# Threshold attention and a feed-forward block: where a group's last addition, the second unit's products, the sums of w_ch1 and the variance stand

## The chip, the cores and the metric

The kernel runs on one core of a Trainium2 chip. The engines are TensorE (PE), VectorE (DVE), ScalarE (ACT), GpSimd (POOL) and SyncE (SP), which issues most DMAs. Each engine takes its instructions in the order in which they were written and waits for others by semaphores. The metric is the device time of one execution in microseconds; lower is better.

## The reference

Eight batches, eight heads, 576 positions, head size 64, all in float32. Attention keeps only the scores within tau of the row's maximum. Its output, with the heads side by side as 512 features, goes through a normalisation and two matrix products with a residual.

```python
scores = scale * np.matmul(q, k.transpose(0, 1, 3, 2))
thresh = np.max(scores, axis=-1, keepdims=True) - tau
scores = np.where(scores >= thresh, scores, -1000000000.0)
attn = np.exp(scores - np.max(scores, axis=-1, keepdims=True))
attn = attn / (np.sum(attn, axis=-1, keepdims=True) + 1e-09)
x = np.matmul(attn, v)          # then (B,H,S,D) -> (B,S,512)
mu = np.mean(x, axis=-1, keepdims=True)
var = np.mean((x - mu) ** 2, axis=-1, keepdims=True)
xn = (x - mu) / np.sqrt(var + 1e-06) * g_ln
out = x + np.maximum(xn @ w_ch1, 0.0) @ w_ch2   # 512 -> 2048 -> 512
```

## The kernel before

**Slots.** Attention runs in 72 slots, nine per batch. A slot makes the scores of one pair of heads (L417, written to the two PSUM tiles sc[0] and sc[1]), their negated row maxima on VectorE (`neg`, L450), thresholds on GpSimd (`thr`, L454), exponentials on ScalarE (`e`, L463), masks with row sums on VectorE (L473), the reciprocal (L478), the division on GpSimd (L490), and transposes on VectorE (L559), whose result goes to DRAM and back by DMAs on SP (`scr`, then `em`). One slot later TensorE multiplies `em` with the values (L638, L649) into the last bank of sc[0] and sc[1], and ScalarE copies that to x (L663).

**Groups.** The feed-forward block works on 16 groups of 288 positions, two per batch: an even one and an odd one. `group_ready` (L1298) files a group's preparation by slot and quarter: the mean, the centring (`centre`, L733, `xc`), the differences t1 to t4 (`sum_x`, L883; t4 on GpSimd), the squares for the variance (L1311) and their additions on GpSimd (L976). `ffn_steps` is a generator that yields after each product; `second_part` (L1249) draws from it in the four quarters of each slot, so that TensorE has feed-forward products between attention's. A yield's first number says where drawing may stop (4: it stops here).

**First product of a group.** `first_units` (L978) computes 2048 features as eight plain tiles (`p1`, one PSUM bank of the pool `ps_ff`, which has two) and two units (`unit`, L901). A unit computes four tiles with seven products instead of eight by sums of w_ch1's blocks, made once by `sums_of_w1` (L862) into `extra` while group 1 is in its second product, and by t1 to t4. Its products go to `chain` (a bank that is added to and copied by ScalarE in between: L929, L942, L948, L958), to `p2` and to two regions of sc[0] called `other`. Their additions on VectorE (L935) wait in `sums_due` until the slot's transposes are written. The two units of a group lie in two slots one after the other. After unit 0 `variance` (L964) writes an averaging product into a bank of its own and spreads it to the 128 partitions by four ScalarE instructions (L716), then Ln and Exp. In an odd group the first of the two slots also turns the next q and k (L355, on VectorE); in an even group the second does.

**Second product of a group.** `second_quarters` (L1072) does it with seven segments. Their additions on VectorE and GpSimd stand in the list `drops`, by name: "11", "21", "22", "u4", "hi" (multiply and add of half of y on GpSimd), "12" (adds the last segment's part p3, on VectorE), "done12" (GpSimd), and the stores. `drip` takes them out in order where a quarter has room; `sum_x` for t4 first takes drops until "12" of the group before is done, as t4 uses that part's buffer.

The pools give a buffer again once its readers are done, and the instruction that writes it waits for them by semaphore.

Of the kernel before, what the change touches and what calls it, by code (L numbers as in the profile page):

```python
# [8 lines left out]
F32 = mybir.dt.float32  # L9
# [3 lines left out]
ALU = mybir.AluOpType  # L13
# [5 lines left out]
def kernel(  # L19
# [31 lines left out]
    nc = tc.nc  # L51
# [5 lines left out]
    NK = DM // 128  # L57
# [646 lines left out]
    def average(to, bank, rhs, start, bias=None):  # L704


        for h in range(2):
            nc.tensor.matmul(
                bank[64 * h : 64 * h + 64], lhsT=avg_sb[:, 64 * h : 64 * h + 64],
                rhs=rhs[:, (early, late)[h]], start=start, stop=True, skip_group_check=True,  # L710
            )

        def spread():
            for at in range(2):
                for h in range(2):
                    nc.scalar.activation(  # L716
                        to[64 * at : 64 * at + 64, (early, late)[h]], bank[64 * h : 64 * h + 64],
                        func=AF.Identity, **({"bias": bias[64 * h : 64 * h + 64]} if bias is not None else {}),
                    )

        return spread
# [29 lines left out]
    def drip(room=None, everything=False):  # L751
# [5 lines left out]
        while drops:  # L757
# [6 lines left out]
            n -= 1  # L764
            go()

    def run_first(calls):
        for fn in calls[:1]:
            calls.pop(0)
            fn()  # L770
# [91 lines left out]
    def sums_of_w1():  # L862


        for k, (f1, f2) in enumerate(UNITS):
            for c in range(2):
                for m in range(2):
                    cols = [slice(128 * t[m], 128 * t[m] + 128) for t in (f1, f2)]
                    a11, a12 = (w1_sb[2 * j + c][:, cols[0]] for j in range(2))
                    a21, a22 = (w1_sb[2 * j + c][:, cols[1]] for j in range(2))  # L870
                    p2, p3, p4 = (piece_of(k, i, c, m) for i in range(3))
                    for eng, out, a, b, op in (
                        (nc.gpsimd, p3, a11, a21, ALU.subtract),
                        (nc.vector, a21, a21, a22, ALU.add),
                        (nc.vector, p2, a21, a11, ALU.subtract),
                        (nc.gpsimd, p4, a12, p2, ALU.subtract),
                    ):
                        eng.tensor_tensor(out=out, in0=a, in1=b, op=op)
                    yield
# [21 lines left out]
    def unit(g, xc, k):  # L901


        f1, f2 = UNITS[k]
        t1, t2, t3, t4 = sums_of_x[g]
        of = lambda f, j: hidden[:, f[0] : f[0] + 2, (early, late)[j]]
        h11, h12, h21, h22 = of(f1, 0), of(f1, 1), of(f2, 0), of(f2, 1)
        w_of = lambda f, j: lambda c, m: w1_sb[2 * j + c][:, 128 * f[m] : 128 * f[m] + 128]
        s_of = lambda which: lambda c, m: piece_of(k, which, c, m)
        x_of = lambda i, j: lambda c: xc[:, 2 * i + c, (early, late)[j]]  # L910
        t_of = lambda t: lambda c: t[:, c]
        other = [
            sc[0][:, 512 * i : 512 * i + TOK].rearrange("p (m t) -> p m t", m=2) for i in range(2)
        ]

        def steps(bank, lhs, rhs, first, last):
            for c in range(2):
                for m in range(2):
                    product(
                        bank[:, m], lhsT=lhs(c, m), rhs=rhs(c),  # L920
                        start=first and c == m == 0, stop=last and c == m == 1,
                        skip_group_check=True,
                    )
                    yield c == m == 1

        chain = ps_ff.tile([128, 2, HT], F32, tag="ff", name="chain")
        for _ in steps(chain, w_of(f1, 0), x_of(0, 0), True, False):
            yield 3, 0.5
        nc.scalar.copy(h12, chain)  # L929
        p2 = ps_ff.tile([128, 2, HT], F32, tag="ff", name="p2")  # L930
        for _ in steps(p2, w_of(f1, 1), x_of(1, 0), True, True):
            yield 3, 0.5

        def add(out, a, b):
            ins = nc.vector.tensor_tensor(out=out, in0=a, in1=b, op=ALU.add)  # L935
            if any(a is t for t in other):
                other_reads.append(ins.ins)

        sums_due.append(lambda: add(h11, p2, h12))
        for end in steps(chain, s_of(0), t_of(t2), False, False):  # L940
            yield 4 if end and part < 2 and now < QUARTERS * NS else 3, 0.5
        nc.scalar.copy(h22, chain)  # L942
        for _ in steps(other[0], w_of(f2, 0), t_of(t1), True, True):
            yield 3, 0.5
        sums_due.append(lambda: add(h12, other[0], h22))
        for _ in steps(chain, s_of(1), t_of(t3), False, False):
            yield 3, 0.5
        nc.scalar.copy(h21, chain)  # L948
        sums_due.append(lambda: add(h22, other[0], h21))
        for end in steps(other[1], s_of(2), x_of(1, 1), True, True):  # L950
            if end:
                sums_due.append(lambda: add(h12, other[1], h12))
            yield 4 if end and now < QUARTERS * NS else 3, 0.5
        for end in steps(chain, w_of(f2, 1), t_of(t4), False, True):
            if not end:
                yield 3, 0.5
        run_all(sums_due)
        nc.scalar.activation(h21, chain, func=AF.Relu)  # L958
        both = hidden[:, f1[0] : f1[0] + 2]
        nc.scalar.activation(both, both, func=AF.Relu)  # L960
        nc.scalar.activation(h22, h22, func=AF.Relu)
        yield 2 if k else 3, 0.5

    def variance(g, sq):  # L964
        x = spare.pop(g)
        bank = ps_ff.tile([128, HT], F32, tag="ff", name="var")
        average(x, bank, sq[:, 0], True, eps_sb)()
        rb = ffn.tile([128, TOK], F32, tag="rb", bufs=2, name="rb")
        nc.scalar.activation(rb, x, func=AF.Ln)
        nc.scalar.activation(rb, rb, func=AF.Exp, scale=-0.5)  # L970
        at_quarter(now // QUARTERS + 1, 3, root, rb, x)
        return rb
# [5 lines left out]
    def first_units(g):  # L978


        xc = centred[g]
        plain, slots = PLAIN[:], unit_slots(g)
        sq = hidden[:, ND - NK :]
        k = 0
        while plain or k < len(UNITS):
            if k < len(UNITS) and (not plain or now // QUARTERS >= slots[k] and part > 1):
                yield from unit(g, xc, k)
                k += 1
                if k == 1:
                    rb = variance(g, sq)  # L990
                    yield 2, 0.5
                continue
            d = plain.pop(0)
            p1 = ps_ff.tile([128, TOK], F32, tag="ff", name="p1")
            for c in range(NK):
                product(
                    p1, lhsT=w1_sb[c][:, d * 128 : (d + 1) * 128], rhs=xc[:, c],
                    start=(c == 0), stop=(c == NK - 1),
                )
                if c < NK - 1:  # L1000
                    yield 1, 1
            nc.scalar.activation(hidden[:, d], p1, func=AF.Relu)  # L1002
            yield 2, 1
        sums_of_x.pop(g)
        return rb
# [229 lines left out]
    def at_quarter(n, i, fn, *args):  # L1235
        later_calls.setdefault((n, i), []).append((fn, args))
# [61 lines left out]
    def group_ready(g):  # L1298
        first = divmod(ready(g), QUARTERS)
        before = divmod(ready(g) - 1, QUARTERS) if g else first  # L1300
        if g == 1:
            at_quarter(*before, lambda: among.append(g))
        else:
            at_quarter(*before, mean_of, g)
            at_quarter(*(first if g and first[1] else before), centre, g)
            if g > 1:
                sq = hidden[:, ND - NK :]
                at_quarter(*before, sum_x, g, (0, 1, 2))
                at_quarter(
                    first[0], -3,  # L1310
                    lambda: nc.scalar.activation(sq, centred[g], func=AF.Square),  # L1311
                )
                at_quarter(first[0], -1, add_squares, sq, 1, 2)
                at_quarter(first[0], 1, add_squares, sq, 3)
                at_quarter(first[0], 1, sum_x, g, (3,))
        at_quarter(*first, lambda: queue.append(ffn_steps(g)))
# [193 lines left out]
```

## Time and profile before

| what | value |
|---|---|
| median of 3 runs | 1337.48 us (1334.98 to 1338.02) |
| the profiled execution's own time | 1336.1 us |
| its span, first to last instruction | 1334.0 us |
| TensorE busy | 1285.2 us, 96% |
| VectorE, GpSimd, ScalarE busy | 947.3, 640.9, 515.0 us |
| granted TensorE clock, mean | 0.997 |

A row of the timeline gives start, duration (both us, from the span's start), engine, line of the kernel, operation, what it writes and reads, shapes, and in brackets the idle time before it and what ended it. Instructions alike that follow each other are one row with a count. Matmuls overlap, and the printed end of one is modelled. A row of the waits gives the waiting engine and line, what it waited for, microseconds in total, how many times, and the longest.

### The profile page before, as it was taken

What the parts mean: (1) busy time and instruction counts of PE and PEld (TensorE: products, weight loads), DVE (VectorE), ACT (ScalarE), POOL (GpSimd) and SP (SyncE); (2) the same over time, 40 slices, a digit from 0 to 9 for tenths busy, and PEclk for the clock granted to TensorE, in tenths of its full rate; (3) what the DMA queues carried; (4) which work ended last, traced back from release to release, by engine and by line L of the source; (5) the groups of instructions that cost most, each with busy time, mean ns of one, the idle gap of its engine ahead of it and who ended that gap; (6) DMA issues with size and microseconds to landing.
All of it is one profiled execution on the core that took longest, in us unless ns stands there. A gap on an engine that the chain in (4) does not pass through costs nothing.

```text
span 1334.0 us, 43429 instructions
## 1 busy us (share of the span) xinstructions
PE 1285.2 (96%) x18648; PEld 1052.7 (79%) x18648; DVE 947.3 (71%) x1714; ACT 515.0 (39%) x1163; POOL 640.9 (48%) x866
## 2 busy tenths in 40 slices
PE   8899899899999999999999999999999999999997
PEld 7765457779788897888879797888978888797977
DVE  7879886676777677777867767776777768676223
ACT  5866332242433424343342424334243433434130
POOL 3465555644445354454634454453544545344323
PEclk9999999999999999999999999999999999999999
DMA  8937765356744665545745566446655466454211
GB/s 155 300 107 187 199 167 182 120 167 193 196 152 148 189 170 169 183 142 148 208 152 188 146 188 194 152 149 189 173 172 178 131 162 186 153 188 143 56 19 19
DMA packets 335311, 214.11 MB, mean 161 GB/s; under 512 B 247376, under 2 KB 292688, under 8 KB 327056
## 3 DMA queue, kind: packets, MB, share of 16 engines
q1 hardware_dynamic: 329008, 210.46, 54.3%
q8 instruction: 146, 2.39, 0.8%
q10 hardware_dynamic: 5952, 0.74, 0.4%
q0 software_dynamic: 160, 0.15, 0.1%
q14 instruction: 45, 0.37, 0.1%
HBM read 124.00 MB, written 87.29 MB: 158 GB/s over the span
## 4 chain that ended last, share of the span: by engine, by line
PE 72%; DVE 8%; POOL 7%; SPq 4%; ACT 4%; issue 3%; DMA 2%; POOLq 0%; DVEq 0%; ACTq 0%
PE seg L103 29%; PE p L103 15%; PE sc L434 9%; PE sc L638 7%; PE chain L103 6%; PE sc L103 3%; POOL e L490 2%; DVE neg L450 2%; ACT e L463 2%; PE sc L649 2%; SPq L120 1%; DVE e L473 1%; DVE extra L569 1%; DVE hidden L935 1%; DVE e L559 1%
## 5 line engine op out<-in xcount | busy, mean ns | idle before, releaser
L103 PE MATMUL p<-xc,w 128*64 128x288 f32 (+1 forms) x2752 | 327.2, 389 | 11.6 <-ACT hidden L958 4.8
L450 DVE TENSOR_REDUCE neg<-sc 128x2 f32<-128x1152 f32 x144 | 189.5, 1353 | 149.8 <-PE sc L434 147.7
L103 PEld LDWEIGHTS p<-xc,w 128*64 128x64 f32 x2752 | 187.7, 137 | 133.4 <-issue 13.5
L490 POOL TENSOR_SCALAR e<-e,den 128x576 f32<-128x576 f32 x264 | 204.5, 788 | 83.5 <-DVE den L478 83.4
L103 PE MATMUL seg<-hidden,w 128*64 128x144 f32 x3840 | 243.9, 287 | 0.0
L103 PEld LDWEIGHTS seg<-hidden,w 128*64 128x64 f32 x3840 | 234.8, 137 | 9.3 <-issue 7.9
L473 DVE SCALAR_TENSOR_TENSOR e<-sc,thr,e 128x576 f32<-128x576 f32 x288 | 222.5, 810 | 12.7 <-POOL thr L454 5.2
L454 POOL TENSOR_SCALAR thr<-neg,low_sb 128x2 f32<-128x2 f32 x144 | 46.3, 322 | 359.2 <-DVE neg L450 358.8
L463 ACT ACTIVATE e<-sc,neg 128x576 f32<-128x576 f32 x288 | 196.6, 752 | 16.4 <-DMA scr<-e 11.9
L559 DVE STREAM_TRANSPOSE e<-e 128x1152 f32<-128x1152 f32 (+1 forms) x113 | 163.8, 1452 | 38.7 <-POOL e L490 37.2
L434 PE MATMUL sc<-kT,qT 64*64 64x384 f32 (+3 forms) x2048 | 139.8, 403 | 1.9 <-DVE e L473 1.9
L638 PE MATMUL sc<-em,v_in 128*64 128x128 f32 (+1 forms) x2368 | 132.7, 267 | 6.4 <-DVE e L473 3.8
L638 PEld LDWEIGHTS sc<-em,v_in 128*64 128x64 f32 x2368 | 124.3, 140 | 9.7 <-issue 3.6
L103 PE MATMUL seg<-hidden,stage 128*64 128x144 f32 x1920 | 124.6, 287 | 0.8 <-ACT part L1117 0.8
L103 PEld LDWEIGHTS seg<-hidden,stage 128*64 128x64 f32 x1920 | 117.4, 137 | 3.8 <-issue 2.5
L434 PEld LDWEIGHTS sc<-kT,qT 64*64 64x64 f32 x2048 | 76.5, 133 | 42.8 <-issue 21.0
L1117 ACT COPY part<-seg 128x288 f32<-128x288 f32 x74 | 29.9, 404 | 183.3 <-PE seg L103 152.2
L663 ACT COPY x<-sc 128x128 f32<-128x128 f32 x120 | 31.3, 265 | 174.9 <-PE sc L434 112.3
L1102 POOL TENSOR_TENSOR hidden<-hidden 128x576 f32<-128x576 f32 x60 | 84.1, 1421 | 29.3 <-ACT hidden L1002 16.8
L1102 DVE TENSOR_TENSOR hidden<-hidden 128x576 f32<-128x576 f32 x60 | 52.5, 904 | 39.4 <-PE seg L103 34.2
L976 POOL TENSOR_TENSOR hidden<-hidden 128x288 f32<-128x288 f32 x48 | 38.7, 807 | 77.9 <-ACT hidden L1311 76.4
L1002 ACT ACTIVATE hidden<-p 128x288 f32<-128x288 f32 x112 | 47.2, 422 | 50.9 <-PE p L103 50.7
(164 smaller groups left out, 1635.3 us busy)
## 6 DMA issues: line engine op xcount, KB each, us to landing
scr<-e SPq DMA_DIRECT2D x60, 1152.0 KB, 5.0
em<-scr SPq DMA_DIRECT2D x63, 1024.0 KB, 5.7
out_dram<-ot SPq DMA_DIRECT2D x248, 36.0 KB, 3.8
q_in<-in_q_dram SPq DMA_DIRECT2D x120, 72.0 KB, 2.6
er<-scr SPq DMA_DIRECT2D x132, 64.0 KB, 5.2
k_in<-in_k_dram SPq DMA_DIRECT2D x116, 72.0 KB, 2.9
v_in<-in_v_dram SPq DMA_DIRECT2D x28, 256.0 KB, 5.6
w<-in_moe_w_ch_dram SPq DMA_DIRECT2D x10, 512.0 KB, 8.3
```

Of the source, the lines that this page charges most:

```text
L103: nc.tensor.matmul(out[r], lhsT=lhsT[:, r], rhs=rhs, **flags)
L434: mm = nc.tensor.matmul(sc[h][64 * i : 64 * i + 64, at : at + n], lhsT=ql[r] if s == HP else qT[r, half, j * 128 + 64 * i : j * 128 + 64 * ...
L450: nc.vector.tensor_reduce(out=neg[:, i], in_=pairs[h], axis=AXL.X, op=ALU.max, negate=True,)
L454: nc.gpsimd.tensor_scalar(out=thr[:, i], in0=neg[:, i], scalar1=-1.0, scalar2=low_sb, op0=ALU.mult, op1=ALU.add,)
L463: nc.scalar.activation(blocks_of(es, i, n), like(blocks[i], n), func=AF.Exp, bias=neg[:, i : i + 1])
L473: nc.vector.scalar_tensor_tensor(out=e, in0=like(blocks[i], n), scalar=thr[:, i : i + 1], in1=e, op0=ALU.is_ge, op1=ALU.mult, accum_out=de ...
L490: nc.gpsimd.tensor_scalar(out=e, in0=e, scalar1=den[:, i : i + 1], scalar2=1.0, op0=ALU.mult, op1=ALU.mult,)
L559: nc.vector.transpose(et[:, :, at], et[:, :, at])
L638: mm = nc.tensor.matmul(dst[64 * h : 64 * h + 64], lhsT=vt[:, h, c, :], rhs=pick(em[:, 2 * j : 2 * j + 2, c], h), start=c == 0 and first, ...
L976: nc.gpsimd.tensor_tensor(out=sq[:, 0], in0=sq[:, 0], in1=sq[:, c], op=ALU.add)
L1002: nc.scalar.activation(hidden[:, d], p1, func=AF.Relu)
L1102: eng.tensor_tensor(out=out[at], in0=in0[at], in1=in1[at], op=op)
```

## The change

There are four edits.

1. `sum_early("12")` is filed at quarter -3 of the slot that follows a group's preparation, ahead of that slot's scores: it takes the addition "12" of the group before out of `drops`, wherever it stands, and issues it there. On VectorE it thereby comes before the slot's two maxima instead of after them (and after the turning of q and k where that is in the slot). `sum_x` for t4 finds it done and takes no drops; on GpSimd t4 and the slot's four divisions now come before "hi". This is so in 13 slots.
2. In the unit with k = 1 the products are issued in the order p5, p6, p3, p7 instead of p6, p5, p7, p3; the additions follow the same order.
3. In `sums_of_w1` the subtraction p3 is on VectorE instead of GpSimd; the last one, p4, stays on GpSimd.
4. Where a plain tile follows unit 0 in the same quarter (`due`; six groups, odd ones), the variance's averaging product goes into the free columns of that tile's bank, between its third and fourth product, and the spreading, Ln and Exp follow that tile's relu on ScalarE. Elsewhere it has a bank of its own as before.

The order of the instructions on SP is the same as before.

```diff
+    def sum_early(what):
+        at = [d[4] for d in drops]
+        if what in at:
+            drops.pop(at.index(what))[-1]()
@@ sums_of_w1
-                        (nc.gpsimd, p3, a11, a21, ALU.subtract),
+                        (nc.vector, p3, a11, a21, ALU.subtract),
                         (nc.vector, a21, a21, a22, ALU.add),
                         (nc.vector, p2, a21, a11, ALU.subtract),
                         (nc.gpsimd, p4, a12, p2, ALU.subtract),
@@ unit
+        def after_p6():
+            nc.scalar.copy(h22, chain)
+            sums_due.append(lambda: add(h12, other[0], h22))
+
+        def after_p7():
+            nc.scalar.copy(h21, chain)
+            sums_due.append(lambda: add(h22, other[0], h21))
+
         sums_due.append(lambda: add(h11, p2, h12))
...
+        p5 = steps(other[0], w_of(f2, 0), t_of(t1), True, True), lambda: None
+        p6 = steps(chain, s_of(0), t_of(t2), False, False), after_p6
+        p7 = steps(chain, s_of(1), t_of(t3), False, False), after_p7
+        p3 = (
+            steps(other[1], s_of(2), x_of(1, 1), True, True),
+            lambda: sums_due.append(lambda: add(h12, other[1], h12)),
+        )
+        order = (p5, p6, p3, p7) if k else (p6, p5, p7, p3)
+        for i, (part_of, after) in enumerate(order):
+            for end in part_of:
+                if end:
+                    after()
+                stop = end and now < QUARTERS * NS and (i == 3 or i == 0 and part < 2)
+                yield 4 if stop else 3, 0.5
@@ variance, first_units
-    def variance(g, sq):
+    def variance(g, spread):
+        spread()
         x = spare.pop(g)
-        bank = ps_ff.tile([128, HT], F32, tag="ff", name="var")
-        average(x, bank, sq[:, 0], True, eps_sb)()
...
                 if k == 1:
-                    rb = variance(g, sq)
-                    yield 2, 0.5
+                    due = plain and owed >= 1
+                    if not due:
+                        bank = ps_ff.tile([128, HT], F32, tag="ff", name="var")
+                        rb = variance(g, average(spare[g], bank, sq[:, 0], True, eps_sb))
+                        yield 2, 0.5
...
             for c in range(NK):
+                if due and c == NK - 1:
+                    spread = average(spare[g], bank[:, TOK : TOK + HT], sq[:, 0], False, eps_sb)
+                    yield 1, 0.5
...
             nc.scalar.activation(hidden[:, d], p1, func=AF.Relu)
+            if due:
+                due = False
+                rb = variance(g, spread)
@@ group_ready
                 at_quarter(*before, sum_x, g, (0, 1, 2))
+                at_quarter(first[0], -3, sum_early, "12")
```

More of the change, by code (lines that the diff above doesn't have):

```diff
@@ L937, in add @@
                 other_reads.append(ins.ins)
-        sums_due.append(lambda: add(h11, p2, h12))
[L940 to L953, printed above, removed]
+        def after_p6():
[4 more added lines that the diff above has]
+            sums_due.append(lambda: add(h22, other[0], h21))
+        sums_due.append(lambda: add(h11, p2, h12))
+        p5 = steps(other[0], w_of(f2, 0), t_of(t1), True, True), lambda: None
[12 more added lines that the diff above has]
+                yield 4 if stop else 3, 0.5
         for end in steps(chain, w_of(f2, 1), t_of(t4), False, True):
@@ L989, in first_units @@
                 if k == 1:
-                    rb = variance(g, sq)
-                    yield 2, 0.5
+                    due = plain and owed >= 1
[3 more added lines that the diff above has]
+                        yield 2, 0.5
                 continue
             d = plain.pop(0)
-            p1 = ps_ff.tile([128, TOK], F32, tag="ff", name="p1")
+            bank = ps_ff.tile([128, 512], F32, tag="ff", name="p1")
+            p1 = bank[:, :TOK]
             for c in range(NK):
+                if due and c == NK - 1:
+                    spread = average(spare[g], bank[:, TOK : TOK + HT], sq[:, 0], False, eps_sb)
+                    yield 1, 0.5
                 product(
@@ L1002, in first_units @@
             nc.scalar.activation(hidden[:, d], p1, func=AF.Relu)
+            if due:
+                due = False
+                rb = variance(g, spread)
             yield 2, 1
```

## The prediction, made before the changed kernel was run

> **What bounds the kernel now.** I read the busy shares first, then TensorE's own waits, then the order in time of each engine in three stretches. TensorE is busy 96% of the span, and the work on it does not change in amount; what can be won is its stalls.
>
> ```profile
> PE 1285.2 (96%) x18648; PEld 1052.7 (79%) x18648; DVE 947.3 (71%) x1714; ACT 515.0 (39%) x1163; POOL 640.9 (48%) x866
> ```
>
> Rows of the waits (waiting engine and line, releaser, us in total, times, longest). The first four are TensorE's; three repeat six or seven times. The last is VectorE's wait for GpSimd in sums_of_w1.
>
> ```profile
> PE p L103 <- ACT hidden L958: 4.8, 7, 0.7
> PE sc L103 <- DVE e L473: 4.3, 6, 0.9
> PE p L103 <- ACT hidden L1002: 2.9, 7, 1.4
> PE chain L103 <- ACT hidden L929: 2.1, 6, 0.3
> ...
> DVE w L878 <- POOL extra L878: 16.4, 7, 5.1
> ```
>
> In time (start, duration, engine): a batch has an even and an odd group. Around the even group's units (425 to 462 us) TensorE shows no idle time. The odd group's two unit slots look like this, first TensorE, then the others:
>
> ```profile
> 504.73 1.15 PE L103 MATMUL chain<-t,extra 128*64 128x144 f32 x16
> 506.55 1.20 PE L103 MATMUL sc<-t,w 128*64 128x144 f32 x16 [0.67 <-DVE e L473]
> ...
> 512.27 0.41 PE L708 MATMUL var<-hidden,avg_sb 128*64 128x144 f32 x4
> 513.40 2.16 PE L103 MATMUL p<-xc,w 128*64 128x288 f32 x16 [0.71 <-ACT hidden L958]
> ...
> 521.20 1.20 PE L103 MATMUL p<-xc,w 128*64 128x144 f32 x16 [0.25 <-ACT hidden L1002]
> 522.75 1.20 PE L103 MATMUL chain<-t,extra 128*64 128x144 f32 x16 [0.35 <-ACT hidden L929]
> ...
> 503.43 1.59 DVE L1142 TENSOR_TENSOR y<-y,part 128x288 f32<-128x288 f32 x1
> ...
> 512.93 0.41 ACT L958 ACTIVATE hidden<-chain 128x288 f32<-128x288 f32 x1 [3.76 <-DVE hidden L935]
> ...
> 503.29 1.42 POOL L1154 TENSOR_TENSOR y<-y,rb 128x576 f32<-128x576 f32 x1
> ```
>
> The printed idle time starts at a modelled end, so I price stalls by starts. Sixteen products of 144 columns follow each other in 0.98 us where nothing waits (502.68 to 503.70 is near it), four in 0.24. Hence (a) the masks: 506.55 - 504.73 - 0.98 = 0.84 us; (b) after the variance: 513.40 - 512.27 - 0.24 = 0.89; (c) 521.20 - 519.80 - 0.98 = 0.42; (d) 522.75 - 521.20 - 0.98 = 0.57. All four recur in the odd groups 3 to 13, six times; one (a) is 0.2 longer. So (a) 5.2, (b) 5.3, (c) 2.5, (d) 3.4 us in all.
>
> The other stalls that the change can reach lie where sums_of_w1 runs, once:
>
> ```profile
> 236.25 3.90 PE L103 MATMUL seg<-hidden,stage 128*64 128x144 f32 x60 [0.76 <-ACT part L1117]
> 241.38 0.34 PE L638 MATMUL sc<-em,v_in 128*64 128x64 f32 x4 [1.23 <-DVE e L473]
> 243.04 3.42 PE L638 MATMUL sc<-em,v_in 128*64 128x64 f32 x60 [1.33 <-DVE e L473]
> ...
> 267.73 4.10 PE L103 MATMUL p<-xc,w 128*64 128x288 f32 x32 [2.37 <-DVE xc L742]
> 273.21 4.10 PE L103 MATMUL p<-xc,w 128*64 128x288 f32 x32 [1.38 <-ACT hidden L1002]
> ...
> 239.23 0.29 DVE L878 TENSOR_TENSOR w<-w,w 128x128 f32<-128x128 f32 x1 [3.74 <-POOL extra L878]
> ```
>
> By starts, with 0.061 us per 144-column product, 0.053 per 64-column one, 0.122 per 288-column one and 2.05 for a slot's scores (begun at 263.24): 0.93 + 1.45 + 1.45 + 2.44 + 1.59 = 7.9 us.
>
> **The change, part by part.**
>
> *w_ch1's sums.* Eight subtractions of 128x128 leave GpSimd (0.46 us each) and join VectorE at 0.29 each, 2.3 us in all. Each stood ahead of VectorE's add, which overwrites its input; VectorE waited 16.4 us for them, because GpSimd took them only after its divisions and hidden differences. Behind the waiting add stood the e transposes, so the scr DMA on SP, so ScalarE's exponentials (at 234.53 they waited 1.47 us for that DMA), so the copy for which TensorE waits at 236.25; and the masks for which it waits at 241.38 and 243.04. Stepping the order through: after the reciprocal at 221.98 VectorE does three sums, then transposes from about 224 to 225 (GpSimd's divisions end at 223.84) instead of 227.62; the exponentials then start near 231.5, and the copy is early: 0.93 gone. The masks start near 234 to 237 instead of 239.77 and end by 237 to 240, TensorE wants them at about 239: of 2.9, 2.2 gone. Later the centring (267.23 before) comes some 1 us before or after it is wanted: of 2.44, 1.9 gone. The last 1.59 follows from the slot's maximum being 2.2 us late behind the first product; VectorE is still about 2 us behind there, as the transposes, five additions, centring and three t differences stand in a row: 0.3 gone. Taken: 5.3. Ends: 0 (VectorE is no later than before; a loss is excluded, as 8 x 0.29 is far below the 16.4 waited) and 7.9.
>
> A row speaks against it: VectorE's y addition took 1.59 us at 503.43 and 0.45 at 427.36, and the long one ran beside GpSimd's y<-y,rb (503.29 to 504.71) and ended 0.3 after it. [...] My 5.3 lets the second group of sums meet one hidden difference (1.4 us).
>
> *The group's last addition* ("12") goes ahead of the slot's two maxima, thirteen times. VectorE idles there for TensorE's scores, 1.24 us in even slots (before 424.82) and 1.71 in odd ones (before 498.86); the copy that it needs ended at 422.96 and 496.99, the t differences at 423.57 and 497.14, so it takes 0.45 us in idle time: nothing. If that cover is gone the maxima, the exponentials, and all masks wait. What it leaves: in odd slots VectorE goes from q_last (503.30 to 503.43) straight to the masks, 1.5 us earlier; the second ends near 504.95, TensorE wants the bank at 505.71: (a) is gone, 5.2 (ends 0 and 5.2). On GpSimd, t4 and the four divisions pass "hi" (1.42 + 1.50): t4 no longer pops it, as "12" is already added. Divisions end near 508.2 instead of 509.93, transposes and the scr DMA follow 1.6 us earlier, and so do unit 0's four sums on VectorE. "hi" and done12 end near 512.8 instead of 511.58; the ot transposes wait for them until then, and VectorE has until about 516. No DMA queue changes its order.
>
> *The variance in p1's bank*, six odd groups. var no longer takes the bank of p2, so p1 takes that one instead of chain's, which ScalarE still had to read (512.93). With the sums earlier that read would begin near 511.6 anyway; both take (b) away: 5.3 (ends 2.6, half, if the p1 bank has a reader as late, and 5.3). TensorE's products stay the same in number. ScalarE now does p1's relu before the four spreads (1.52), Ln and Exp (0.88), ending about 0.5 us into the next slot's first x copy; the second maximum, which waits for that copy, is due 0.5 us later: nothing. The bank is free again (spreads near 515.8) 2 us before chain asks.
>
> *The second unit's order*, fourteen times: p5 before p6 and p3 before p7. Even groups lose nothing: the masks of sc[0] end at 450.2, p5 would start at 451.63. In odd groups p6 no longer waits for the copy of chain (ready 522.7), but p5 waits for the second mask, whose accumulator is read out at 522.41 to 522.49. So p5 starts near 522.55 instead of p6 at 522.75: 0.2 x 6 = 1.2 (ends -0.6, if the mask comes 0.3 later than before, and 3.4). (c) stays: ScalarE's relu stands between exponentials, tied to the scores (ends 0 and 2.5).
>
> **Sum.** 5.3 + 5.2 + 5.3 + 1.2 = 17.0. Against the profiled execution's 1336.1 us: 1319.1. The median shown, 1337.48, is 1.4 above it, the lowest run 1.1 below, so I forecast 1319. All low ends: 0 + 0 + 2.6 - 0.6 = 2, 1334; all high: 7.9 + 5.2 + 5.3 + 3.4 + 2.5 = 24.3, 1312.
>
> **The rivals.**
>
> 1. *Everything reachable goes*, (c) and (d) too: 1312. For it: two earlier stalls move the whole of ScalarE's work. Against: (c) and (d) are timed from the same slot's scores.
> 2. [...]
> 3. *A wait takes the place of (a) or (b)*: chain's next product waits for a copy, or p1's bank for ScalarE, and only half of these 10.5 comes: 5.3 + 5.3 + 1.2 = 11.8, and with the sums' gain halved 9, 1327.
> 4. *Slower: the addition delays the maxima.* It decides from the point where it ends after the scores, that is 0.8 us later than I place it in even slots, for which the last segment's copy on ScalarE must be late or the addition last 1.59 under GpSimd's squares (from 424.10). With maxima 2.2 us late TensorE loses 1.59 at the third product group (the 273.21 row). Thirteen times that is 20.7, (a) stays too; 11.8 - 20.7 = 9 us slower, 1345. Against: GpSimd is idle there until 424.10 and 498.13.
> 5. *Nothing*: the stalls only move, 1336.
>
> **How the numbers follow.** Forecast (1314 to 1324 with its own range) 0.52, rival 1 0.12, rival 2 0.17, rival 3 0.09, rival 4 0.07, rival 5 0.03. A difference under 0.2% (2.7 us) can't be told from no change here. Faster 0.52 + 0.12 + 0.17 + 0.09 = 0.90; same 0.03; slower 0.07. The range 1310 to 1328 leaves out rivals 4 and 5 and the upper part of 3, and goes 2 us below rival 1, since runs differ by 3 us.
>
> **What would show it.** Right: the rows of VectorE waiting for GpSimd in the sums gone; TensorE's wait for the masks gone in odd slots; no wait of p for L958's successor; chain's wait replaced by one of sc for masks near 0.2 us; the y addition at 0.45. Wrong: maxima that no longer start 0.1 us after the scores, masks still later than 239 us in the stretch of sums, or a new TensorE wait for p1's bank.

## The result, and the profile after

The changed kernel takes 1317.41 us (median of 4 runs, 1316.66 to 1318.11) beside 1337.75 us for the kernel before (4 runs, 1334.98 to 1338.16): a ratio of 0.9852, 95% interval 0.9835 to 0.9869, 20.3 us faster. Run once more on another occasion beside 15 runs of before it took 1319.52 us, ratio 0.9862 [0.9849, 0.9876]. The forecast was 1319 with a range of 1310 to 1328.

The profiled execution of the changed kernel took 1317.26 us with a span of 1315.4; before it was 1336.1 and 1334.0. The spans differ by 18.6 us, and the comparison below is made inside these two executions unless another is named.

The busy times of the whole span, after:

```profile
PE 1280.6 (97%) x18648; PEld 1050.7 (80%) x18648; DVE 948.3 (72%) x1722; ACT 515.0 (39%) x1163; POOL 638.2 (49%) x858
```

The matmuls are the same 18648 in number; eight instructions have gone from POOL to DVE (866 to 858, 1714 to 1722). TensorE's busy time is 4.6 us less although its work is the same, a first hint that products ran faster somewhere (the section on why the forecast was right says where). The rows of the waits on TensorE that answer to those of before (engine, line, releaser: us in total, times, longest):

```profile
PE p L103 <- ACT hidden L1022: 2.9, 7, 1.4
...
PE sc L103 <- DVE e L473: 0.9, 6, 0.2
PE seg L103 <- ACT y L1140: 0.6, 2, 0.4
...
PE chain L103 <- ACT hidden L949: 0.5, 1, 0.5
PE p L103 <- ACT hidden L971: 0.5, 1, 0.5
```

Read them against the four rows of before. ScalarE's read of chain (L958 before, L971 now) held up p seven times for 4.8 us and does so once, in the last group. The masks (DVE e L473) cost 4.3 us and cost 0.9, and these 0.9 are another product than before: p5 of the second unit, 0.15 each. The wait for the plain tile's relu (L1002 before, L1022 now) is unchanged at 2.9. The chain wait, 2.1 in six pieces, is gone from the odd groups; the 0.5 at chain in the last group is a new one. The row of VectorE waiting for GpSimd in sums_of_w1 (16.4 us) is gone altogether. Two waits of `seg` for a copy have come in that this execution of before does not show; e2_sums says more of them.

The odd group's two unit slots in time, TensorE (start, duration, operation, and idle time before it with its releaser in brackets):

```profile
495.35 1.15 PE L103 MATMUL chain<-t,extra 128*64 128x144 f32 x16
496.33 1.15 PE L103 MATMUL sc<-t,w 128*64 128x144 f32 x16
...
502.00 1.62 PE L103 MATMUL p<-xc,w 128*64 128x288 f32 x12
503.46 0.41 PE L708 MATMUL p<-hidden,avg_sb 128*64 128x144 f32 x4
503.70 0.66 PE L103 MATMUL p<-xc,w 128*64 128x288 f32 x4
...
509.99 1.20 PE L103 MATMUL p<-xc,w 128*64 128x144 f32 x16 [0.25 <-ACT hidden L1022]
511.35 1.20 PE L103 MATMUL sc<-t,w 128*64 128x144 f32 x16 [0.15 <-DVE e L473]
```

(a) 496.33 - 495.35 = 0.98: no wait for the masks. (b) the four averaging products stand inside p1 and all follow without idle time. (c) unchanged. (d) 511.35 - 509.99 - 0.98 = 0.38 instead of 0.57, now on the second mask. VectorE at the same slot's begin:

```profile
487.69 0.45 DVE L1165 TENSOR_TENSOR y<-y,part 128x288 f32<-128x288 f32 x1
489.48 2.62 DVE L450 TENSOR_REDUCE neg<-sc 128x2 f32<-128x1152 f32 x2 [1.34 <-PE sc L434]
```

The addition takes 0.45 us (1.59 before, at its old place), in idle time, and 1.34 us of idle time are still left ahead of the maxima, which start 0.1 us after the scores end (489.38). In the first of the 13 slots it is otherwise. VectorE is behind there, has no idle time, and the maxima come after the addition, 2.25 us after the scores end (260.34):

```profile
262.22 0.45 DVE L1165 TENSOR_TENSOR y<-y,part 128x288 f32<-128x288 f32 x1
262.59 2.61 DVE L450 TENSOR_REDUCE neg<-sc 128x2 f32<-128x1152 f32 x2
```

The stretch of the sums, TensorE:

```profile
231.71 7.76 PE L103 MATMUL seg<-hidden,stage 128*64 128x144 f32 x124
239.52 2.08 PE L638 MATMUL sc<-em,v_in 128*64 128x64 f32 x64
...
260.34 4.10 PE L103 MATMUL p<-xc,w 128*64 128x288 f32 x32
265.87 4.10 PE L103 MATMUL p<-xc,w 128*64 128x288 f32 x32 [1.42 <-ACT hidden L1022]
269.80 1.15 PE L103 MATMUL chain<-xc,w 128*64 128x144 f32 x16
```

Four of the five stalls are gone; the copy no longer splits the 124 products, nor the masks the 64. The fifth is left whole: 265.87 - 260.34 - 3.93 = 1.60 (32 products of 288 columns take 3.93 us by starts where nothing waits, as 265.87 to 269.80 shows).

Where the 18.6 us came from, by four stretches of the two executions: from the span's start to the scores at 227.09 (227.40 after) -0.3 (a second execution of the changed kernel, e9_after_again, has these scores at 228.28, so this much comes and goes by itself); from there to the chain's first product at 277.14 (269.80 after) 50.05 against 42.40, +7.65; from there to the product that waits for the last group's xc (1268.50, 1249.60) +11.56; from there to the end 65.5 against 65.8, -0.3.

### The profile page after: what moved, and what is told of

It is laid out like the page before. It is cut to its first block, busy times and chain, and to the rows that moved or that the text cites. A ratio compares the mean times of both kernels' runs of the same rounds, so it can differ in the third digit from the quotient of the medians.

```text
span 1315.4 us, 43423 instructions
## 1 busy us (share of the span) xinstructions
PE 1280.6 (97%) x18648; PEld 1050.7 (80%) x18648; DVE 948.3 (72%) x1722; ACT 515.0 (39%) x1163; POOL 638.2 (49%) x858
## 4 chain that ended last, share of the span: by engine, by line
PE 74%; DVE 3%; POOL 1%; DMA 1%; ACT 1%; issue 1%; POOLq 0%; DVEq 0%; ACTq 0%
PE seg L103 28%; PE p L103 16%; PE chain L103 8%; PE sc L434 8%; PE sc L638 7%; PE sc L103 4%; PE sc L649 2%; DVE e L473 1%; DMA scr<-e 1%; DVE neg L450 1%; POOL sum L692 0%; DVE e L559 0%; POOL thr L454 0%; PE mean L708 0%; POOL e L490 0%
## 5 line engine op out<-in xcount | busy, mean ns | idle before, releaser
L473 DVE SCALAR_TENSOR_TENSOR e<-sc,thr,e 128x576 f32<-128x576 f32 x288 | 222.3, 809 | 15.6 <-POOL thr L454 8.6
L1022 ACT ACTIVATE hidden<-p 128x288 f32<-128x288 f32 x112 | 47.2, 422 | 56.0 <-PE p L103 55.9
```

The costliest lines, as they stand in the source:

```text
L473: nc.vector.scalar_tensor_tensor(out=e, in0=like(blocks[i], n), scalar=thr[:, i : i + 1], in1=e, op0=ALU.is_ge, op1=ALU.mult, accum_out=de ...
```

## The experiments

The first four kernels change one thing each in the kernel before (1337.31 us, 15 runs beside them); the others start from the changed kernel. They were run on three occasions; across occasions the ratios to before compare better than the times.

### e1_early: the kernel before with the early addition alone

```diff
+    def sum_early(what):
+        at = [d[4] for d in drops]
+        if what in at:
+            drops.pop(at.index(what))[-1]()
...
                 at_quarter(*before, sum_x, g, (0, 1, 2))
+                at_quarter(first[0], -3, sum_early, "12")
```

> Only the early addition of "12". Theory: it takes away (a), 5.2 us over the six odd groups, and about half of (b): ScalarE's last read of chain then begins when TensorE's product ends (as in the changed kernel, 502.22 against a product ending at 502.0) and no longer after VectorE's late sums, so p1 still waits about 0.44 us instead of 0.89. That is 5.2 + 2.7 = 7.9 us, about 1329.8 against 1337.7. Rival: (b) hangs on the bank alone and stays 0.89, so 5.2 us, about 1332.5. The stalls in the stretch of w_ch1's sums stay as they were (7.9 us) by both.

1330.07 us (1328.38 to 1331.79), ratio 0.9939 [0.9927, 0.9952]: 7.2 us faster. TensorE in an odd group:

```profile
504.75 1.15 PE L103 MATMUL sc<-t,w 128*64 128x144 f32 x16
...
510.41 0.41 PE L708 MATMUL var<-hidden,avg_sb 128*64 128x144 f32 x4
511.10 2.16 PE L103 MATMUL p<-xc,w 128*64 128x288 f32 x16 [0.27 <-ACT hidden L963]
```

The idle time before the first line is gone, as is (a). In the last line (b) is 511.10 - 510.41 - 0.24 = 0.45 us instead of 0.89. So the addition takes (a) and half of (b): since VectorE comes earlier to the unit's sums, ScalarE's read of chain begins earlier. 6 x (0.84 + 0.44) = 7.7 is what the rows give, 7.2 what was measured; the 5.2 of (a) alone lies below the interval (6.4 us at its low end). In the first slot the addition costs a little: the last stall of the sums' stretch is 273.57 - 267.73 - 3.93 = 1.91 us here and 1.55 in before.

### e2_sums: w_ch1's p3 on VectorE alone

```diff
-                        (nc.gpsimd, p3, a11, a21, ALU.subtract),
+                        (nc.vector, p3, a11, a21, ALU.subtract),
```

> Only the subtraction p3 on VectorE. Theory: the stretch of sums gains 7.6 us, as the two traces differ by 50.05 against 42.40 us from the scores at 227 us to the first chain product: the stalls of 0.93, 1.45, 1.45 and 2.44 us go, 1.6 stays, and 1.4 us more comes from products that ran at half the granted clock after the two stalls of 1.45 (clock 0.78, 0.50 and 0.86 in 242 to 248 us of the kernel before). About 1330. Rival: the stalls in that stretch were shortened by the other edits too, and this alone gives the 5.3 us of the forecast or less, 1332.4. All stalls in odd groups stay.

1329.89 us (1329.11 to 1331.22), ratio 0.994 [0.9928, 0.9953]: 7.4 us. The scores at 227.19 and the chain's first product at 269.13 are 41.94 us apart (50.05 before); only the last stall of the stretch is left, and the odd groups keep all of theirs. The stretch alone gives 8.1 us; one wait, which before does not show, takes 1.6 of it back. The last stall, then that wait:

```profile
265.20 4.10 PE L103 MATMUL p<-xc,w 128*64 128x288 f32 x32 [1.24 <-ACT hidden L1002]
...
855.77 2.51 PE L103 MATMUL seg<-hidden,stage 128*64 128x144 f32 x37 [1.01 <-ACT y L1117]
```

It comes twice (1.01 and 0.57 us). In the changed kernel the same wait is 0.36 and 0.25; there the copy stands behind an exponential that had waited 1.19 us for the scr DMA. Every kernel here but before shows it in its profile, with 0.2 to 1.6 us in all, and two executions of the changed kernel have 0.6 and 1.5. So it is not the work of one edit, and what sets it was not isolated.

### e3_var: the variance in p1's bank alone

The `due` branch of the change, without the early addition, with the old order and with p3 on GpSimd.

> Only the variance in p1's bank. Theory: p1 takes p2's bank and no longer waits for ScalarE's last read of chain although that read is as late as before: (b) goes wholly, 5.3 us, about 1332.4; (a) stays 0.84 us. Rival: the late read of chain delays ScalarE's relu, spreads, Ln and Exp into the next slot, so that the second maximum or the first tile there is late and what is won comes back as a new wait: nothing, 1337.7.

1331.83 us (1331.05 to 1332.18), ratio 0.9952 [0.994, 0.9965]: 5.5 us. (b) is gone and (a) stays:

```profile
505.52 1.20 PE L103 MATMUL sc<-t,w 128*64 128x144 f32 x16 [0.67 <-DVE e L473]
...
512.69 0.41 PE L708 MATMUL p<-hidden,avg_sb 128*64 128x144 f32 x4
512.94 0.66 PE L103 MATMUL p<-xc,w 128*64 128x288 f32 x4
```

This step needs no help from the other: the bank alone removes the whole of (b).

### e4_order: the second unit's order alone

```diff
-        order = (p6, p5, p7, p3)
+        order = (p5, p6, p3, p7) if k else (p6, p5, p7, p3)
```

> Only the order of the second unit's products. Theory: in the six odd groups the wait of 0.57 us for chain's copy becomes one of about 0.37 us for the second mask: 1.2 us won. In the last group, where no attention product stands between p7 and the product after it, TensorE waits for the copy of chain after p7, which p3 covered before: 0.7 us lost. Sum 0.5 us, not to be told from no change, 1337.2. Rival: the masks come late where the early addition is not there, and p5 waits longer than p6 did, a loss of up to 6 x 0.3 + 0.7 = 2.5 us, 1340.

1337.73 us (11 runs, 1336.98 to 1339.87), ratio 1.0003 [0.9994, 1.0012]: no gain. Yet in the trace (d) shrinks as forecast, to an idle time of 0.15 for the mask. Two things are set against these 6 x 0.19 = 1.1 us: the last group has the new chain wait of 0.50 (see e6_tail), and the `seg` waits of e2_sums take 0.9. The expectation's 0.5 us could not be told from nothing either way. One more thing is seen in this execution. The stall that the kernel before also has at 267.73 is followed by slower products:

```profile
268.12 7.15 PE L103 MATMUL p<-xc,w 128*64 128x288 f32 x44 [2.35 <-DVE xc L742]
```

44 such products take 44 x 0.1225 + 0.17 = 5.6 us elsewhere. The 1.6 us more is what a stretch at a granted clock of 0.50 costs in other runs (1.4 to 1.7 us, the last section). It cost nothing here, as the wait for the plain tile's relu behind it fell away in exchange: from the scores (227.46) to the chain's first product (277.53) it is 50.07 us, and 50.05 in before.

### e5_no_early: the changed kernel without the early addition

> The changed kernel without the early addition of "12" alone. Theory: the early addition and the variance's place share (b), which the variance takes whole by itself; so without the early addition only (a) comes back, 0.84 us in six odd groups, 5.0 to 5.2 us, no wait for chain's last reader: about 1322.5. Rival: the two add up, and 7.2 us (what the early addition gave alone) come back, 1324.6.

1322.7 us (1321.49 to 1323.52), ratio 0.9882 [0.9865, 0.9899]. The changed kernel did not run beside it: its two times lie 5.3 and 3.2 us below, its two ratios 0.0030 and 0.0020 (4.0 and 2.7 us). The traces say more: (a) is back in every odd group, and p1 waits for nothing.

```profile
498.62 1.20 PE L103 MATMUL sc<-t,w 128*64 128x144 f32 x16 [0.67 <-DVE e L473]
...
505.80 0.41 PE L708 MATMUL p<-hidden,avg_sb 128*64 128x144 f32 x4
506.04 0.66 PE L103 MATMUL p<-xc,w 128*64 128x288 f32 x4
```

From the chain's first product (270.34) to the last group's xc wait (1255.47) it is 985.13 us, and 979.80 in the changed kernel: 5.3 more without the addition. But the stretch before it, from the scores to the chain, is 41.93 without it (41.94 in e2_sums) and 42.28 to 42.40 in the four profiled executions with it and with the sums as in the change. So the addition costs 0.4 us in the first slot, and by these traces it is worth about 4.9 us as the last step (the `seg` waits of e2_sums are alike in the two, 0.7 and 0.6), against 7.2 measured alone: the bank takes (b) anyway.

### e6_tail and e10_tail_again: the last group as it was, with its variance in p1's bank

```diff
-        order = (p5, p6, p3, p7) if k else (p6, p5, p7, p3)
+        order = (p5, p6, p3, p7) if k and g < NG - 1 else (p6, p5, p7, p3)
...
-                    due = plain and owed >= 1
+                    due = plain and (owed >= 1 or g == NG - 1)
```

The last group of the changed kernel, TensorE:

```profile
1265.14 2.16 PE L103 MATMUL p<-xc,w 128*64 128x288 f32 x16 [0.46 <-ACT hidden L971]
1267.48 6.04 PE L103 MATMUL p<-xc,w 128*64 128x288 f32 x48 [0.18 <-ACT sum L716]
...
1278.25 1.15 PE L103 MATMUL chain<-t,extra 128*64 128x144 f32 x16
1279.90 1.20 PE L103 MATMUL chain<-t,w 128*64 128x144 f32 x16 [0.50 <-ACT hidden L949]
```

In other groups the attention's `sc<-em,v_in` (1.75 us) stands between p7 (1278.25) and p4 (1279.90), and ScalarE copies chain behind it. Here nothing stands there, and the new order puts the copy straight between the two: 1279.90 - 1278.25 - 0.98 = 0.67 us. In the old order p3 covered it. The waits of 0.46 and 0.18 are not new; before has them too, at 1284.05 and 1286.39.

> The changed kernel with two edits for the last group alone, behind whose units no attention product stands: its second unit in the old order, and its variance in the next plain tile's bank. Theory: the wait of 0.50 us (0.67 by starts) at the last product of chain goes, and so do those of 0.46 and 0.18 (0.62 and 0.4 by starts) after the variance: 1.7 us, 1315.7. Rival: the last group's end hangs on VectorE's additions or the stores, and the time stays 1317.4.

1316.69 us (1315.68 to 1317.15), ratio 0.9837 [0.9821, 0.9854]. Repeated beside the changed kernel on the same chip, with this expectation for the changed kernel itself (e9_after_again, no edit):

> The changed kernel once more, beside the two versions of its end and the middle delay: 1317 us, ratio 0.985 of before; every account expects the same, it is the measure for the next three.

> The changed kernel whose last group keeps the old order of the second unit and takes the variance in p1's bank. By the traces the stretch from the last group's xc wait to the end is 1.3 us shorter than in the changed kernel, so 1.3 us below it, 1315.7. Rival: the waits of 0.50, 0.46 and 0.18 us are taken up by a later wait at the very end, no difference.

e9_after_again took 1319.52 us (1318.04 to 1320.47), e10_tail_again 1316.59 (1316.2 to 1318.22), ratios 0.9862 [0.9849, 0.9876] and 0.9844 [0.983, 0.9857]. The last group of e10_tail_again:

```profile
1266.27 0.41 PE L708 MATMUL p<-hidden,avg_sb 128*64 128x144 f32 x4
1266.52 6.69 PE L103 MATMUL p<-xc,w 128*64 128x288 f32 x52
...
1278.92 1.15 PE L103 MATMUL chain<-t,w 128*64 128x144 f32 x16
```

The three waits are gone. From the xc wait to the end it is 1314.8 - 1250.15 = 64.65 us, against 65.8 and 66.1 in the two profiled executions of the changed kernel: 1.2 to 1.5 us shorter. The medians differ by 2.9 us in this comparison and the two intervals overlap a little; 1.2 to 1.5 is what the traces explain.

### e11_tail_sums: the same, with the parts of w_ch1's sums spread otherwise

```diff
-            if i % 13 == 12:
+            if i % 11 == 6:
                 next(sums, None)
```

> The same, and sums_of_w1 takes a part at every eleventh step from the sixth on, not at every thirteenth from the twelfth. Theory: the stall of 1.6 us that stays at 265.87 us comes from VectorE being about 2.2 us behind with the sums that stand between 247 and 255 us; with these sums done earlier (some in the 4.7 us that VectorE idles before 215.82) it goes in part, 0.8 to 1.6 us less than the tail version, 1314.5. Rival: the masks that TensorE wants at 239.5 us come late instead, because more sums stand ahead of them, and 0 to 2 us are added.

1315.7 us (1314.26 to 1316.89), ratio 0.9834 [0.9821, 0.9848], the fastest kernel here, yet not told apart from e10_tail_again. TensorE:

```profile
235.20 3.90 PE L103 MATMUL seg<-hidden,stage 128*64 128x144 f32 x60 [0.43 <-ACT part L1140]
239.47 2.09 PE L638 MATMUL sc<-em,v_in 128*64 128x64 f32 x64 [0.38 <-DVE den L478]
...
260.36 4.10 PE L103 MATMUL p<-xc,w 128*64 128x288 f32 x32
265.13 4.10 PE L103 MATMUL p<-xc,w 128*64 128x288 f32 x32 [0.67 <-ACT hidden L1022]
```

Both accounts came true at once. The last stall falls to 265.13 - 260.36 - 3.93 = 0.84, and the two stalls that the change had removed at the copy and the masks come back in small. From the scores (226.37) to the chain's first product (269.06) it is 42.69 us, against 42.32 in e10_tail_again: nothing is won in this stretch. The sums were not moved into the idle time before 215.82; they met GpSimd's divisions and hidden differences instead, and one pair took 2.15 us (222.65) and a single one 1.40 (224.83), beside one of 1.39 (234.60) that the changed kernel has too (1.40 at 233.75).

### e7_pad4, e12_pad10 and e8_pad15: a delay of the maxima

These test the slower rival, that the addition delays the maxima. Four and fifteen were run first, and ten to part the two explanations that fifteen left open. n small transposes of a spare tile stand on VectorE between the early addition and the slot's maxima; nothing else reads them.

```diff
                 at_quarter(first[0], -3, sum_early, "12")
+                for _ in range(n):
+                    at_quarter(first[0], -3, nc.vector.transpose, pad, pad)
```

> The changed kernel with four transposes of 128x64 of a spare tile put between the early addition and the two maxima in VectorE's queue, some 0.8 us of extra work in each of the 13 slots. Theory (the point from which the forecast's slower rival decides lies 0.8 us late in even slots, 1.3 in odd ones): the maxima start no later than the scores end, nothing is lost, 1317.4 to 1318. Rival: there is no such slack on VectorE, each slot's maxima are 0.8 us late and TensorE loses 0.3 to 0.6 us in each, 1321 to 1325.

> Ten transposes of a spare 128x64 tile (0.27 us each, 2.7 us) between the early addition and the slot's maxima, instead of fifteen (4.07 us, 1365.0 us) or four (1320.1 us). Theory that a part of the 4.2 us per even slot with fifteen is a halved TensorE clock after a stall of 2.54 us, and that a shorter stall does not halve it: even slots stall 2.54 - 1.35 = 1.2 us with the granted clock at 1.00 after it, odd slots 2.6 - 1.35 = 1.25; with the first slot's 2.7 + 1.7 = 4.4 this is 6 x 1.2 + 6 x 1.25 + 4.4 = 19 us over the changed kernel, 1336. Rival, that the loss follows the delay alone, one us for one us: 6 x (4.2 - 1.35) + 6 x 1.25 + 4.4 = 29 us, 1346.

> As before with 15 transposes, some 2.8 us of extra work in each of the 13 slots: the maxima come about 2 us late in even slots and 1.5 in odd ones. Theory: a late maximum makes ScalarE's exponentials late, with the relus of the plain tiles behind them, and TensorE waits for the bank at its third product group, as it does once at 265.87 us (1.6 us by starts with maxima 2.25 us late): 1.0 to 1.6 us in each slot, 13 to 21 us in all, 1330 to 1338, as slow as the kernel before. Rival: VectorE and ScalarE catch up within the slot and TensorE, with its feed-forward products in between, loses under 0.3 us in each: under 1322.

| n | delay on VectorE | us | ratio, 95% |
|---|---|---|---|
| 0 | 0 | 1317.41, 1319.52 | 0.9852, 0.9862 |
| 4 | 1.0 us | 1320.1 | 0.9864 [0.9844, 0.9884] |
| 10 | 2.7 us | 1337.78 | 0.9998 [0.9989, 1.0007] |
| 15 | 4.1 us | 1365.0 | 1.0199 [1.0182, 1.0216] |

VectorE in an even slot with four:

```profile
416.74 0.45 DVE L1167 TENSOR_TENSOR y<-y,part 128x288 f32<-128x288 f32 x1
417.11 1.08 DVE L1265 STREAM_TRANSPOSE pad<-pad 128x64 f32<-128x64 f32 x4
418.11 2.58 DVE L452 TENSOR_REDUCE neg<-sc 128x2 f32<-128x1152 f32 x2
```

The scores end at 417.97 there: VectorE was done with the early addition 0.86 us before them (417.11), and 1.0 us more just reaches the edge. By time e7_pad4 can't be told from the changed kernel (1320.1 against 1317.41 and 1319.52). In even slots the theory of its expectation held, but neither account had the first slot. What it loses by its trace lies in one place, the first slot at 266.80, where the maxima are late in the changed kernel too: 1.15 us more of stall (266.80 - 260.12 - 3.93 = 2.75 instead of 1.60) and 1.7 us of slower products behind it. With ten, TensorE in an even and an odd slot:

```profile
420.88 4.10 PE L105 MATMUL p<-xc,w 128*64 128x288 f32 x32
425.95 4.10 PE L105 MATMUL p<-xc,w 128*64 128x288 f32 x32 [0.97 <-ACT hidden L1024]
...
500.72 1.20 PE L105 MATMUL chain<-xc,w 128*64 128x144 f32 x16 [0.51 <-ACT hidden L1024]
502.29 1.20 PE L105 MATMUL p<-xc,w 128*64 128x144 f32 x16 [0.36 <-ACT hidden L1024]
```

By starts the even slot stalls 425.95 - 420.88 - 3.93 = 1.14 us with maxima 1.82 us late (422.70), and the odd slot 0.68 + 0.59 = 1.27, with the granted clock at 1.00 behind both (426 to 432 and 502 to 506 us). Six batches of 2.41 and 5.2 in the first slot make 19.7; the spans differ by 18.6 (16.5 against e9_after_again's), and the median lies 18.3 above e9_after_again's, which ran beside it. So the theory's 19 us held and the rival's 29 did not. Thus 2.7 us of VectorE time ahead of the maxima would have eaten the whole gain of the change. With fifteen both accounts of the expectation were far too low (1338 at most, 1365.0 measured): a transpose took 0.27 us and not the 0.19 assumed, so that the maxima were 3.2 us late and not 2. The stalls are 2.54 and 2.67 us, but a batch grows by 6.7 to 8.6 us and not by the 5.2 of the stalls. The difference is the clock, which was granted at 0.50 in 432 to 434 us and in 831 to 833: a drop costs 1.69 us in an even slot (32 products in 5.62 us by starts instead of 3.93) and 1.50 in an odd one, and each of the five batches that can be compared has one or both.

## Why the forecast was right, step by step

**The w_ch1 sums: forecast 5.3, measured 7.65.** The mechanism held: transposes at 224.31 (forecast 224 to 225), masks at 235.07 (234 to 237), both ahead of TensorE's want. The exponentials came at 233.31, later than the 231.5 forecast, having waited 2.10 us for the scr DMA, and were still in time. The term was sized too low in two places. The forecast kept 0.7 of the masks' 2.9 us and 0.5 of the 2.44 at the centring; both went whole, which makes 0.93 + 2.90 + 2.44 = 6.27. It took 0.3 off the last stall, which did not move (1.55 to 1.60): without the early addition it is 1.41 (e2_sums), and the addition, late in that slot, puts this back. The other 1.4 us were never in the list of stalls: after the two stalls of 1.45 us TensorE ran at half speed, as the stretches of 2 us in before show (busy us and number of instructions of each engine, then PEclk, the granted clock, DMA share and GB/s):

```profile
242.00:244.00 2.00, 0.96 (x18) 0.96 (x20) 1.15 (x5) 0.00 (x0) 1.82 (x4) 0.78 0.00 0
244.00:246.00 2.00, 2.00 (x43) 2.00 (x42) 0.77 (x3) 0.00 (x0) 1.27 (x4) 0.50 0.00 0
246.00:248.00 2.00, 2.00 (x47) 1.80 (x46) 2.00 (x2) 0.40 (x1) 0.77 (x2) 0.86 0.03 8
```

The 60 products that began at 243.04 were followed 3.20 us later by the next operation; after the change all 64 take 1.89, at a clock of 1.00. A stall's price can go on after the stall, in the duration column and not in the idle column. The forecast had the row of 3.42 us for 60 products in view and read only the bracket behind it. Its "0.053 per 64-column" product is even taken from this row (3.20 / 60) and is the half-speed price; at full speed it is 1.89 / 64 = 0.0295, and 60 x (0.0533 - 0.0295) is the 1.4.

**The longer times beside GpSimd, of which the 1.59 row spoke,** came, and cost less than the change won. VectorE in after, beside GpSimd's divisions (221.29 to 224.25) and then alone:

```profile
222.20 0.69 DVE L883 TENSOR_TENSOR extra<-w 128x128 f32<-128x128 f32 x1
...
232.09 0.28 DVE L883 TENSOR_TENSOR extra<-w 128x128 f32<-128x128 f32 x1
```

All 24 sums took 11.6 us instead of 24 x 0.29 = 7.0, so 4.6 us went to running beside GpSimd: 0.69 to 0.75 for a sum beside its divisions, 0.45 beside its own sums, and one met a hidden difference (1.40), as assumed. That is about 0.2 us for a sum. VectorE no longer waits 16.4 us for GpSimd, and TensorE shows no stall from it before 262 us. That nothing would be won in this stretch, which had the 0.17 of rival 2, no run shows: e2_sums won 7.4 us by itself.

**The early addition: forecast 5.2, by the traces about 4.9** as the last step (e5_no_early), 7.2 measured alone (e1_early). (a) went whole, as forecast. The cover, 0.45 us in idle time, held in 12 of the 13 slots, with 0.88 us of idle time (even) or 1.34 (odd) left behind it. "Nothing" for all 13 was wrong for the first, where VectorE was still behind from the sums: the addition delayed the maxima there and cost 0.4 us. The forecast itself had VectorE 2 us behind at that place, in its paragraph on the sums.

**The variance: forecast 5.3, measured 5.5** alone. Of the two that were to take (b), the bank takes the whole of it (e3_var, e5_no_early) and the earlier sums alone only half (e1_early). Rival 3, a wait in their place, is excluded by the profile: p1 waits for nothing between 502 and 504 us.

**The second unit's order: forecast 1.2, in the trace 6 x 0.19 = 1.1, by time nothing alone** (e4_order, where the `seg` waits took 0.9 as well). What failed is "fourteen times" with one account for all: the last group has no attention product between p7 and p4, and pays 0.67. The forecast looked at the even and the odd group and not at the last.

**(c) stays**, 0.25 of idle time as before, and so does most of (d); with that rival 1 (1312) is out.

**The slower rival** had its point of decision right: 0.8 us later than placed, and e7_pad4 found 0.86. Its price of 1.59 for maxima 2.2 us late agrees with the rows of e12_pad10 and e8_pad15, where the stall is the lateness less 0.7 (1.82 late, 1.14; 3.2 late, 2.54). It did not happen, but for the 0.4 us in the first slot, because in the other twelve the addition ended ahead of the scores.

**The sum.** 17.0 was forecast and 18.6 measured between the two spans: 7.65 + 11.56 - 0.3 at the start, which no step of the change explains, - 0.3 at the end. The six batches shrink by 2.01 us each where no new wait stands (155.37 to 153.36), 12.0 in all (forecast 5.2 + 5.3 + 1.2 = 11.7); the two new `seg` waits, which were not forecast, take about half a microsecond of it. So one term was forecast 2.35 us too low, and losses that the forecast did not see (the last group's copy, the `seg` waits) took part of this back. That the total is out by only 1.6 us is in part luck.

## What to carry to other kernels

Price a stall by starts, and look at the duration and the granted clock of the work behind it as well as at the idle time ahead of it (in before, 1.4 us of slower products at a clock of 0.50). Work that is put into an engine's idle time is free only up to the edge that the trace shows: here 0.9 us in even slots, 1.3 in odd ones and none in the first, and 2.7 us would have cost all that the change won. When an edit repeats in every round of a loop, read the first and the last round by themselves, since what covers it elsewhere may be missing there; and do not add up the gains of two edits that remove the same wait.

## What the runs showed of the hardware that was not expected

Behind some stalls TensorE's granted clock is 0.50 (in before in 244 to 246 us, in e8_pad15 in 432 to 434), at a cost of 1.4 to 1.7 us that no row of waits holds (2.4 in e12_pad10's first slot, nothing in e4_order, where it took the place of a wait). How long it lasts can be estimated from the clocks of the stretches of 2 us, if the clock is either 0.50 or 1.00. In before it is (0.22 + 0.50 + 0.14) x 2 / 0.5 = 3.4 us. In e8_pad15, with 0.51 and 0.64 in 592 to 596, it is (0.49 + 0.36) x 2 / 0.5 = 3.4. In e12_pad10's first slot, with 0.95, 0.50, 0.50, 0.50 and 0.84 in 264 to 274, it is (0.05 + 0.50 + 0.50 + 0.50 + 0.16) x 2 / 0.5 = 6.8, twice as much, and the stall is longer there. The stalls (idle time printed, us) and the first products behind them (time printed, us), across the runs:

| kernel, place | idle before | products behind it |
|---|---|---|
| before, 241.38 and 243.04 | 1.23 and 1.33 | slower: 60 in 3.42, clock 0.50 in 244 to 246 |
| before, 267.73 | 2.37 | full speed: 32 in 4.10, clock 1.00 |
| e4_order, 268.12 | 2.35 | slower: 44 in 7.15 |
| e7_pad4, 266.80 | 2.58 | slower: 32 in 5.79 |
| e12_pad10, 267.80 | 4.26 | slower: 32 in 6.46, clock 0.50 in 266 to 272 |
| e8_pad15, 271.07 | 5.7 | slower: clock 0.50 in 270 to 274 |
| e8_pad15, six even slots | 2.36 to 2.37 | 32 in 5.79 in three, in 4.10 in three |
| e8_pad15, six odd slots | 1.91, then 0.36 to 0.37 | full speed in three (16 in 1.20, clock 1.00), slower in three (16 in 2.19, clock 0.50 to 0.60) |
| e12_pad10, even and odd slots | 0.97; 0.51, then 0.36 | full speed: 32 in 4.10, 16 in 1.20, clock 1.00 |

Two even slots of e8_pad15 with the same stall, TensorE:

```profile
751.88 5.79 PE L105 MATMUL p<-xc,w 128*64 128x288 f32 x32 [2.36 <-ACT hidden L1024]
...
913.83 4.10 PE L105 MATMUL p<-xc,w 128*64 128x288 f32 x32 [2.36 <-ACT hidden L1024]
```

The same 32 products after the same 2.36 us of idle time take 5.79 us in one batch and 4.10 in another. So the length of the stall alone does not decide. Whether it is the moment at which the stall falls, or the work before it, the runs don't part. A stall of 2.35 us (e4_order), and two of 1.45 us by starts close together (before), were enough for slower products; one of 2.37 us (before, 267.73) was not. What decides was not measured.
